# Expert 1's last twelve chunks, taken two by two over 768 tokens, with the first product by Strassen's algorithm

## The chip, the cores and the metric

The kernel runs on one core of one Trainium2 chip. The metric is the device time of one execution in microseconds (us); lower is better. Matrix products run on TensorE (PE in the profile), whose results land in eight PSUM banks of 128 x 512 floats. VectorE (DVE) and ScalarE (ACT) read and write the banks and SBUF. SyncE (SP) issues the transfers. On this kernel a change of less than 0.2% (1.2 us) can't be told from none.

## The reference

```python
x = attention(q, k, v)                 # 2 batches x 8 heads x 768 positions, head size 64
x = x.transpose(0, 2, 1, 3).reshape(1536, 512)
h = x @ w_in                           # expert 1: 512 -> 2048
x2 = (h * tanh(softplus(h))) @ w_out   # Mish, 2048 -> 512
a, b = x2 @ w_a, x2 @ w_b              # expert 2: 512 -> 1536, twice
return (a * b) @ w_out2                # 1536 -> 512
```

Each query attends to the keys less than 16 positions away and to 24 block summaries (maximum of the keys, mean of the values, over 32 positions). The weights come as 64-bit floats.

## The kernel before

Attention goes in 24 batches: six granules of 256 tokens by four pairs of heads. A granule of finished attention output is a piece of x. It is kept as two fp32r tiles, XH (rounded) and XL (what the rounding left), and so is every operand of the experts: a product w·x is three matmuls, wh·xh, wl·xh and wh·xl.

Expert 1 has 16 chunks of 128 hidden columns. A step (`step1`) takes one chunk for one block of tokens: 12 matmuls give h in one bank (L903), ACT makes Mish of it in SBUF (L932), a cast and a DVE subtraction (L388, L935) split the result, and 12 matmuls (L950) add to y, which stays in its four banks over all chunks of a visit. `visits1` gives the blocks of a visit and its chunks:

```python
visits1 = [((0,), 0, NG1), ((1,), 0, NG1), ((2,), 0, NG1),          # NG1 = 5
           ((3,), 0, NC1), ((2,), NG1, NC1), ((0, 1), NG1, NC1)]    # NC1 = 16
```

Blocks 0 and 1 have 256 tokens, blocks 2 and 3 have 512. So the chunks from 5 on come when much of attention is done, and each is used three times with 512 tokens. Converted weights stay in 26 slots of SBUF.

A weight tile (128 x 512) arrives as raw 64-bit halves. `convert` puts fp32 together from them: an ACT instruction (L685 or L688), DVE's shift L690, DVE's L693 and, where ACT's form is the unsigned one (L688), DVE's L697. `split` then needs an ACT cast (L388) and a DVE subtraction (L705).

Expert 2 already goes by Strassen's algorithm: for two 128-column products over half of the tokens (768, one batch), seven products of combined operands, six matmuls of 384 columns each (L1044), take the place of eight. Weight combinations come from DVE (L736), token combinations are made once per half (`combine_x`), and the seven results are put together by three ACT copies (L1052) and DVE operations on the banks (L1055). `expand` (L1105) is the last product, added up in SBUF by L1121.

No loop sets the order in which the engines work: all instructions are given to a planner (class `Plan`) with a key, the time at which each is due, and it writes out one order for each engine by keys, by readiness, by its own table of costs and by which banks are free. `pace` and the other constants are such keys. `tc.manual_schedule()` keeps that order.

Of the kernel before, what the change touches and what calls it, by code (L numbers as in the profile page):

```python
# [19 lines left out]
CELL = 32  # L20
# [212 lines left out]
def attention_mish_moe_bilinear_moe(  # L233
# [35 lines left out]
    n_blk = [GT, GT, 2 * GT, 2 * GT]  # L269
    t_blk = [0, GT, 2 * GT, 4 * GT]  # L270
    gran_blk = [(0, 0), (1, 0), (2, 0), (2, GT), (3, 0), (3, GT)]
# [5 lines left out]
    TOT, N_BASE, N_EXT = 53184, 16, 10  # L277
# [23 lines left out]
    NQ, NSA, NAT, NST, NT = 2, 4, 2, 3, 3  # L301
    XH = [take(KC * n) for n in n_blk]
    XL = [take(KC * n) for n in n_blk]
    G_HL = [take(1024) for _ in range(2)]
    base_slots = [take(1024) for _ in range(N_BASE)]
# [4 lines left out]
    kt_o = [take(SK) for _ in range(NP)]  # L310
    T_S = [take(512) for _ in range(NT)]
    T_L = [take(512) for _ in range(NT)]
    X2 = [Y0 + KC * GT * i for i in range(6)]
    assert Y1 == X2[1] and kt_o[0] == X2[2] and T_L[0] == T_S[0] + NT * 512
    TMP = X2[5] + KC * GT
    TN = 384
    tmp_o = [TMP + TN * i for i in range((T_L[-1] + 512 - TMP) // TN)]
# [15 lines left out]
    n_ext = max(top[0] - EXT, TOT - EXT, 1024 * N_EXT)  # L333
    assert EXT + n_ext <= TOT, EXT + n_ext
    ext_slots = [EXT + 1024 * i for i in range(N_EXT)]
# [3 lines left out]
    gran2 = {(0,): [0], (1,): [1], (2,): [2, 3], (3,): [4, 5], (0, 1): [0, 1]}  # L339
    XC = [{}, {}]  # L340
    XN = ("B11", "B21", "T2", "T1", "T3", "B22", "T4")

    def chunks(regions):
        out, rest = [], []
        for o, n in regions:
            while n >= 2 * TN:
                out.append((o, o + TN))
                o, n = o + 2 * TN, n - 2 * TN
            if n >= TN:
                rest.append(o)  # L350
        return out + list(zip(rest[0::2], rest[1::2]))

    SL = base_slots
    x_regions = [[(XH[0], 2048), (XL[0], 2048), (SL[3], 7 * 1024)], [(XH[2], 4096), (XL[2], 4096), (SL[0], 3 * 1024)]]
    assert XH[1] == XH[0] + 1024 and XL[1] == XL[0] + 1024 and XH[3] == XH[2] + 2048 and XL[3] == XL[2] + 2048
    for p_, rg in enumerate(x_regions):
        ch = chunks(rg)
        assert len(ch) >= 2 * len(XN), len(ch)
        for i_, nm in enumerate(XN):
            XC[p_][nm] = (ch[2 * i_], ch[2 * i_ + 1])  # L360

    b0, e0 = SL[10], EXT
    W2 = [b0, e0, e0 + 3584]
    O2 = [e0 + 7168 + 1024 * i for i in range(3)]
    PH = [G_HL[0], G_HL[0] + 768] + [b0 + 3584 + 768 * i for i in range(3)] + [e0 + 10240]
    assert b0 + 3584 + 3 * 768 <= SL[-1] + 1024 and n_ext >= 10240 + 768 and G_HL[1] == G_HL[0] + 1024

# [234 lines left out]
    def batch_o(key, g, ps):  # L602
# [60 lines left out]
        hk, lk = ([sb(X[blk] + p * n + t0, GT) for p in ps] for X in (XH, XL))  # L663
# [541 lines left out]
```

## Time and profile before

| | |
|---|---|
| median of 3 runs | 612.4 us (612.25 to 612.71) |
| profiled execution | 611.92 us, of which the span (first to last instruction) is 610.2 us |
| mean granted TensorE clock | 0.991 |
| PE busy | 597.1 us (98%) |
| PE weight loads busy | 525.4 us (86%) |
| DVE busy | 411.2 us (67%) |
| ACT busy | 295.9 us (48%) |

The busy shares are means over stages that differ: up to about 117 us attention and expert 1 are mixed, then come expert 1 alone (to 330 us) and expert 2. Busy time of neighbouring instructions overlaps, since one starts before the one ahead has finished; what an instruction costs its engine in a row is therefore the distance from its start to the next start. Lines are those of the kernel before; in the changed kernel the same code stands at other lines (L903 is L877 there, L950 is L923, L932 is L906, L935 is L909, L690, L693, L697 are L670, L673, L677, L705 is L685, L736 is L712, L634 is L615, L665 is L645, L1044 is L1052, L1105 is L1165).

### The profile page before, as it was taken

To read this page: it belongs to the slowest core of one execution; us is meant where nothing else is said; L and a number is where in the kernel's file an instruction comes from. 1 tells how busy PE (TensorE), PEld (TensorE's weight loads), DVE (VectorE), ACT (ScalarE), POOL (GpSimd) and SP (SyncE) were. 2 spreads that over 40 slices of the span, in tenths; PEclk is the share of its full clock that TensorE was granted. 3 is DMA by queue.
4 is the path that set the end of the run, shared out by engine and by line. 5 is a ranking of instruction groups with operands and counts; after the bars stand their busy time and mean duration, and the time that the engine had idled before them with its cause. 6 is when DMAs were issued, how large, how long until landed. Compare 5 with 4: busy or idle time off the path is not lost.

```text
span 610.2 us, 10411 instructions
## 1 busy us (share of the span) xinstructions
PE 597.1 (98%) x4119; PEld 525.4 (86%) x4119; DVE 411.2 (67%) x946; ACT 295.9 (48%) x648; POOL 6.8 (1%) x34
## 2 busy tenths in 40 slices
PE   7899999999999999999999999999999999999996
PEld 4688998888888888888888999999999999999995
DVE  5989999989831111148678865539879769656456
ACT  4889988766522322136356445345544524422210
POOL 3000000000000000000000000000000000000000
PEclk8979999999999999999999999999999999999999
DMA  8998432455500000001132012112342222000005
GB/s 301 337 317 271 143 102 71 144 196 172 180 1 0 1 0 1 1 1 40 64 119 89 1 35 70 36 69 70 105 137 70 69 70 71 0 35 1 0 1 207
DMA packets 20638, 54.87 MB, mean 90 GB/s; under 512 B 1805, under 2 KB 4877, under 8 KB 20589
## 3 DMA queue, kind: packets, MB, share of 16 engines
q1 hardware_dynamic: 20588, 54.21, 26.7%
q8 instruction: 32, 0.52, 0.4%
q14 instruction: 18, 0.14, 0.1%
HBM read 50.07 MB, written 3.15 MB: 87 GB/s over the span
## 4 chain that ended last, share of the span: by engine, by line
PE 90%; ACT 4%; DVE 2%; DMA 2%; issue 0%; SPq 0%; DVEq 0%; ACTq 0%
PE bank L1044 29%; PE bank L950 21%; PE bank L903 20%; PE bank L1105 16%; PE bank L634 2%; ACT attn L590 2%; PE bank L563 1%; PE bank L622 1%; DMA attn<-in_qT_dram 1%; ACT arena L688 1%; PE bank L567 1%; DMA out_dram<-arena 1%; ACT rounded L388 1%; DVE attn L584 0%; ACT L932 0%
## 5 line engine op out<-in xcount | busy, mean ns | idle before, releaser
L388 ACT CAST rounded<-arena 128x512 fp32r<-128x512 f32 (+3 forms) x139 | 82.4, 606 | 93.0 <-PE bank L950 40.3
L1044 PE MATMUL bank<-rounded,wext 128*128 128x384 f32 x672 | 120.4, 335 | 0.0
L1044 PEld LDWEIGHTS bank<-rounded,wext 128*128 128x128 f32 x672 | 117.1, 188 | 1.3 <-ACT arena L1052 0.5
L950 PE MATMUL bank<-rounded 128*128 128x512 f32 (+1 forms) x456 | 98.0, 364 | 0.0
L903 PE MATMUL bank<-rounded 128*128 128x512 f32 (+1 forms) x456 | 96.0, 363 | 0.5 <-ACT arena L932 0.5
L935 DVE TENSOR_TENSOR rounded<-arena,rounded 128x512 fp32r<-128x512 f32 (+1 forms) x53 | 33.8, 638 | 85.2 <-ACT rounded L388 85.0
L903 PEld LDWEIGHTS bank<-rounded 128*128 128x128 f32 x456 | 77.6, 189 | 14.4 <-ACT arena L932 0.7
L950 PEld LDWEIGHTS bank<-rounded 128*128 128x128 f32 x456 | 77.9, 189 | 13.7 <-issue 0.2
L1105 PE MATMUL bank<-wext,rounded 128*128 128x512 f32 x360 | 87.4, 390 | 0.0
L1055 DVE TENSOR_TENSOR arena<-arena,bank 128x384 f32<-128x384 f32 x96 | 52.6, 551 | 39.5 <-PE bank L1044 30.4
L1105 PEld LDWEIGHTS bank<-wext,rounded 128*128 128x128 f32 x360 | 67.4, 188 | 13.4
L705 DVE TENSOR_TENSOR rounded<-arena,rounded 128x512 fp32r<-128x512 f32 (+3 forms) x92 | 59.4, 658 | 5.7 <-ACT rounded L388 4.0
L1044 PE MATMUL bank<-rounded 128*128 128x384 f32 x336 | 61.1, 335 | 0.0
L1052 ACT COPY arena<-bank 128x384 f32<-128x384 f32 x72 | 34.3, 481 | 53.9 <-PE bank L1044 51.7
L1044 PEld LDWEIGHTS bank<-rounded 128*128 128x128 f32 x336 | 58.7, 188 | 0.6
L388 ACT CAST wext<-arena 128x512 fp32r<-128x512 f32 (+2 forms) x62 | 37.7, 615 | 43.3 <-DVE arena L1075 11.0
L932 ACT ACTIVATE arena<-bank 128x512 f32<-128x512 f32 (+1 forms) x53 | 29.4, 557 | 53.3 <-PE bank L903 53.2
L693 DVE SCALAR_TENSOR_TENSOR arena<-arena 128x512 uint32<-128x512 uint32 x68 | 47.0, 691 | 6.6 <-ACT arena L688 2.2
L1121 DVE TENSOR_TENSOR arena<-bank,arena 128x512 f32<-128x512 f32 x60 | 40.4, 687 | 14.1 <-PE bank L1105 13.5
L903 PE MATMUL bank<-rounded,wext 128*128 128x512 f32 x180 | 43.2, 389 | 0.0
L950 PE MATMUL bank<-rounded,wext 128*128 128x512 f32 x180 | 43.2, 389 | 0.0
L705 DVE TENSOR_TENSOR wext<-arena,wext 128x512 fp32r<-128x512 f32 (+2 forms) x62 | 38.7, 634 | 5.1 <-PE bank L950 2.5
(73 smaller groups left out, 566.9 us busy)
## 6 DMA issues: line engine op xcount, KB each, us to landing
arena<-in_w_out_dram SPq DMA_DIRECT2D x28, 512.0 KB, 3.3
arena<-in_w_in_dram SPq DMA_DIRECT2D x16, 512.0 KB, 4.2
arena<-in_w_a_dram SPq DMA_DIRECT2D x12, 512.0 KB, 3.2
arena<-in_w_b_dram SPq DMA_DIRECT2D x12, 512.0 KB, 3.7
arena<-in_kT_dram SPq DMA_DIRECT2D x8, 384.0 KB, 6.6
attn<-in_v_dram SPq DMA_DIRECT2D x4, 768.0 KB, 6.3
out_dram<-arena SPq DMA_DIRECT2D x12, 256.0 KB, 3.1
attn<-in_qT_dram SPq DMA_DIRECT2D x5, 512.0 KB, 6.1
```

What stands on the lines that cost most here:

```text
L388: alts = [("ACT", act_us(n), lambda env: nc.scalar.copy(out=dst(env), in_=src(env))), ("DVE", dve2_us(n) if fast else dve_us(n), lambda en ...
L693: dve(key, 512, lambda env: nc.vector.scalar_tensor_tensor(out=f.bitcast(U32), in0=hw.bitcast(U32), scalar=3, in1=f.bitcast(U32), op0=ALU. ...
L705: dve(key, n, lambda env: nc.vector.tensor_sub(out=r32(lo[0]()), in0=src, in1=hi[0]()), r=rd + hi[1], w=lo[1])
L903: nc.tensor.matmul(like(dst, b), lt, rt, start=(j == 0), stop=(j == 3 * KC - 1))
L932: act(ka, n, lambda env: nc.scalar.activation(out=g, in_=hp(env), func=AF.Mish), w=[hn, sb(lo, n)], free=[hn], table="mish")
L935: dve(ka, n, lambda env: nc.vector.tensor_sub(out=r32(gl), in0=g, in1=gh), r=[sb(lo, n), sb(ho, n)], w=[sb(go, n)])
L950: nc.tensor.matmul(yp, lt, r32(rt), start=(fst and j == 0), stop=(lst and j == 2))
L1044: nc.tensor.matmul(dst, lt, rt, start=(start and i == 0 and j == 0), stop=(last and i == 1 and j == 2), skip_group_check=True)
L1052: act(k, TN, lambda env: nc.scalar.copy(out=dst[0], in_=bank[env[nm[z]]][:, 0:TN]), w=[nm[z]] + dst[1])
L1055: dve(k, TN, lambda env: op(out=dst[0], in0=dst[0], in1=bank[env[nm[z]]][:, 0:TN]), w=dst[1] + [nm[z]], free=[nm[z]] if free else [])
L1105: nc.tensor.matmul(dst, lt, rt, start=(j == 0), stop=(j == n - 1))
L1121: dve(kf, 512, lambda env, acc=acc, ot=ot, on=on: nc.vector.tensor_add(ot, bank[env[on]], acc), r=ak, w=[on] + ok, free=[on])
```

## The change

Chunks 0 to 3 of expert 1 are still done block by block (`NG1 = 4`, four visits). Chunks 4 to 15 are done afterwards in pairs, for each pair first all 768 tokens of batch 0 (A), then all of batch 1 (B): twelve steps `step_l`. In each, h of both chunks comes from the routine for seven products that expert 2 uses (now `strassen`); four tiles of 128 x 384 go through Mish and are split; y comes in eight groups of six matmuls (both chunks, 384 tokens), and each group is added by DVE (L1128) to X2 in SBUF instead of waiting in a bank. The combinations of x that the seven products read are made by `combine_x1` (L974, L977) before the first step. Weights aren't kept: `prep_pair` prepares a pair of w_in chunks with Strassen's sums, double-buffered, and w_out goes through four slots. The choice between the two forms of `convert` goes by `SIGN`: the signed form early and late, the unsigned one (with the third DVE instruction) in between. Expert 2's order begins with half A instead of B.

```diff
-    NG1 = 5
-    visits1 = [((0,), 0, NG1), ((1,), 0, NG1), ((2,), 0, NG1), ((3,), 0, NC1), ((2,), NG1, NC1), ((0, 1), NG1, NC1)]
+    NG1 = 4
+    visits1 = [((0,), 0, NG1), ((1,), 0, NG1), ((2,), 0, NG1), ((3,), 0, NG1)]
-    pace = (6.2, 3.4, 5.2, 5.2, 5.2, 5.2)
+    pace = (6.2, 4.6, 6.0, 5.4)
+    D1 = 15.6
+    for cp in range(NG1, NC1, 2):
+        for p_ in (0, 1):
+            seqL.append((cp, p_, tl))
+            tl += D1
-        return w_first[c] > t + 20.0
+        return key < SIGN[0] or key > SIGN[1]
+    SIGN = (T0 + 20.0, tl + 20.0)
+    def step_l(cp, p_, ts):
+        e = IN[(cp - NG1) // 2 % 2]
...
+        def mish(nm, k, src, rd, o, free=()):
...
+            copy(k, TN, lambda env: r32(ar(o, TN)), lambda env: g, fast=True, r=gk, w=[sb(o, TN)])
+            dve(k, TN, lambda env: nc.vector.tensor_sub(out=r32(ar(o + TN, TN)), in0=g, in1=ar(o, TN)),
...
+        _, _, _, xn, _ = strassen(tag, p_, e, ts, d, out)
+        mish("21", ts + 7 * d, lambda env: bank[env[xn]][:, 0:TN], [xn], tmp(), free=[xn])
...
+        for j, (th, m) in enumerate((th, m) for th in (1, 0) for m in range(KC)):
...
+                for c, go, wa in pair:
...
+                    for lt, rt in ((wh, gh), (wl, gh), (wh, gl)):
+                        nc.tensor.matmul(bank[env[yn]][:, 0:TN], lt, rt, start=(q == 0), stop=(q == 5))
...
+            dve(k + 1.0, TN, lambda env, acc=acc, yn=yn: nc.vector.tensor_add(
+                acc, bank[env[yn]][:, 0:TN].rearrange("p (g n) -> p g n", g=3), acc), w=[yn] + ak, free=[yn])
+    combine_x1(A_, t - 16.0)
+    combine_x1(B_, t - 1.0)
+    for cp, p_, ts in seqL:
...
+            prep_pair(IN[i % 2], ts - (10.0 if i else 8.0), ("in", cp), ("in", cp + 1))
+            for c in (cp, cp + 1):
+                load_w(ts + 2.0 + 2.0 * (c - cp), "out", c, OUT[c % 4])
+        step_l(cp, p_, ts)
+    combine_x2(A_, tl - 10.0)
+    combine_x2(B_, tl + 12.0)
```

What this does to the orders is seen at three places. The first is TensorE around the last attention matmuls (the last AV product is the row on attn with 64x64). Before:

```order
L950 MATMUL bank_64<-rounded 128x512 x3
L950 MATMUL bank_67<-rounded 128x512 x3
L634 MATMUL bank_65<-attn 64x64 x16
L950 MATMUL bank_62<-rounded 128x512 x3
L950 MATMUL bank_63<-rounded 128x512 x3
L950 MATMUL bank_64<-rounded 128x512 x3
L903 MATMUL bank_68<-rounded 128x512 x12
```

In the changed kernel the same place reads:

```order
L615 MATMUL bank_65<-attn 64x64 x16
L923 MATMUL bank_66<-rounded 128x512 x3
L923 MATMUL bank_68<-rounded 128x512 x3
L923 MATMUL bank_61<-rounded 128x512 x3
L923 MATMUL bank_63<-rounded 128x512 x3
L877 MATMUL bank_67<-rounded 128x512 x12
```

and 120 matmuls of 512 columns after it, the first of the seven products begin:

```order
L923 MATMUL bank_68<-rounded 128x512 x3
L923 MATMUL bank_61<-rounded 128x512 x3
L1052 MATMUL bank_63<-rounded,wext 128x384 x6
L1052 MATMUL bank_62<-rounded,wext 128x384 x6
L1052 MATMUL bank_64<-rounded,wext 128x384 x6
L1052 MATMUL bank_65<-rounded,wext 128x384 x6
L1052 MATMUL bank_64<-rounded,wext 128x384 x6
```

Ahead of the last AV row stand 240 matmuls of 256 columns and 93 of 512 (L903, L950) before, 192 and 72 now. Behind it stand 939 of 512 and 1008 of 384 before, 120 and 2088 now, and 432 of L1105 (L1165) in both.

The second place is VectorE up to the subtraction that takes the last attention output from its bank (L665, now L645). Before, weight conversion stands there:

```order
L690 TENSOR_SCALAR arena<-arena 128x512
L693 SCALAR_TENSOR_TENSOR arena<-arena 128x512
L697 SCALAR_TENSOR_TENSOR arena<-arena 128x512
L705 TENSOR_TENSOR rounded<-arena,rounded 128x512
L665 TENSOR_TENSOR rounded<-bank_68,rounded 128x2x256
L705 TENSOR_TENSOR rounded<-arena,rounded 128x512
...
L665 TENSOR_TENSOR rounded<-bank_65,rounded 128x2x256
```

Now the combinations of x for half A stand there:

```order
L645 TENSOR_TENSOR rounded<-bank_62,rounded 128x512
L977 TENSOR_TENSOR arena<-rounded 128x384
L974 TENSOR_TENSOR rounded<-arena,rounded 128x384
L977 TENSOR_TENSOR arena<-arena 128x384 x2
L370 CAST rounded<-arena 128x512
L977 TENSOR_TENSOR arena<-arena 128x384
L909 TENSOR_TENSOR rounded<-arena,rounded 128x512
L974 TENSOR_TENSOR rounded<-arena,rounded 128x384
L974 TENSOR_TENSOR rounded<-arena,rounded 128x3x128
L645 TENSOR_TENSOR rounded<-bank_65,rounded 128x512
```

Counted over all rows from the start to this one, the changed VectorE has 7 fewer of L690, 9 fewer of L693, 17 fewer of L697 (none is left), 8 fewer of L705 and 2 fewer 256-column L935, and 23 more of 384 columns (L974, L977); it also has seven more casts and copies of 512 columns. ScalarE, counted up to its last cast of attention output, has four more table loads (15 for 11, and one at the start in both), 6 fewer weight conversions, 15 fewer casts and copies of 512 columns, 8 more casts of 384 and 3 fewer Mish.

The third place is TensorE in the steady part of the pairs, where a product and a y group alternate, each in a bank of its own:

```order
L1052 MATMUL bank_68<-rounded,wext 128x384 x6
L1121 MATMUL bank_65<-rounded,wext 128x384 x6
L1052 MATMUL bank_61<-rounded,wext 128x384 x6
L1121 MATMUL bank_63<-rounded,wext 128x384 x6
L1052 MATMUL bank_68<-rounded,wext 128x384 x6
L1121 MATMUL bank_62<-rounded,wext 128x384 x6
```

Before, twelve L903 and twelve L950 alternated here, and no bank was read between the steps but that of h.

## Rows read from the trace of the kernel before

**Rows 1.** The page: span, busy time of each engine, chain by engine.

```profile
span 610.2 us, 10411 instructions
PE 597.1 (98%) x4119; PEld 525.4 (86%) x4119; DVE 411.2 (67%) x946; ACT 295.9 (48%) x648; POOL 6.8 (1%) x34
PE 90%; ACT 4%; DVE 2%; DMA 2%; issue 0%; SPq 0%; DVEq 0%; ACTq 0%
```

**Rows 2.** The chain of waits, longest pieces: start us, us, what ran.

```profile
55.02 1.89 ACT attn L590 x10
58.64 1.28 ACT L932
60.38 1.70 PE bank L903 x12
62.08 1.44 PE bank L950 x12
...
116.12 1.08 PE bank L634 x32
117.20 2.27 PE bank L950 x9
119.46 2.72 PE bank L903 x12
...
308.50 5.44 PE bank L903 x24
...
330.26 28.16 PE bank L1044 x162
...
520.57 14.64 PE bank L1044 x84
...
601.75 3.23 DMA out_dram<-arena
```

**Rows 3.** Windows: stretch, its length, each engine's busy us (instructions), clock.

```profile
30.00:40.00 10.00, 8.09 (x148) 7.07 (x151) 9.19 (x21) 8.33 (x24) 0.00 (x0) 0.66 1.01 322
80.00:90.00 10.00, 10.00 (x131) 9.00 (x124) 10.00 (x50) 8.92 (x36) 0.52 (x1) 1.00 0.48 137
100.00:120.00 20.00, 20.00 (x167) 16.44 (x162) 19.04 (x54) 17.09 (x44) 0.00 (x0) 1.00 0.31 107
120.00:160.00 40.00, 40.00 (x178) 33.14 (x177) 36.03 (x65) 25.64 (x44) 0.00 (x0) 1.00 0.52 171
400.00:500.00 100.00, 100.00 (x523) 92.89 (x522) 80.99 (x161) 46.18 (x86) 0.00 (x0) 1.00 0.24 80
```

**Rows 4.** VectorE's timeline, three stretches: start us, busy us, instruction.

```profile
127.51 0.42 DVE L690 TENSOR_SCALAR arena<-arena 128x512 uint32<-128x512 uint32 x1
127.84 0.69 DVE L697 SCALAR_TENSOR_TENSOR arena<-arena 128x512 uint32<-128x512 uint32 x1
128.44 0.69 DVE L693 SCALAR_TENSOR_TENSOR arena<-arena 128x512 uint32<-128x512 uint32 x1
...
405.53 0.55 DVE L705 TENSOR_TENSOR rounded<-arena,rounded 128x384 fp32r<-128x384 f32 x1
405.99 0.55 DVE L1055 TENSOR_TENSOR arena<-arena,bank 128x384 f32<-128x384 f32 x1
406.46 1.29 DVE L705 TENSOR_TENSOR wext<-arena,wext 128x512 fp32r<-128x512 f32 x2
...
412.79 0.42 DVE L736 TENSOR_TENSOR arena<-arena 128x256 f32<-128x256 f32 x1
413.13 0.55 DVE L1075 TENSOR_TENSOR arena<-arena 128x384 f32<-128x384 f32 x1
```

**Rows 5.** ScalarE's timeline around a table load.

```profile
41.83 0.59 ACT L388 CAST rounded<-bank 128x512 fp32r<-128x512 f32 x1 [0.63 <-PE bank L634]
42.44 1.28 ACT L590 ACT_TABLE_LOAD   x1
43.73 0.40 ACT L590 ACTIVATE attn<-attn 128x120 f32<-128x120 f32 x1
```

More of the change, by code (lines that the diff above doesn't have):

```diff
@@ L299, in ar @@
         return a
[L301 to L305, printed above, removed]
+    NQ, NSA, NAT, NST, NT, SPARE = 2, 4, 2, 3, 3, 832
+    NG2 = S // GT * B
+    XH = [take(KC * GT) for _ in range(NG2)]
+    XL = [take(KC * GT) for _ in range(NG2)]
+    TE = [take(9 * 512) for _ in range(2)]
+    EW = [take(1024) for _ in range(8)]
+    G_HL = [TE[1], TE[1] + 1024]
     RND = top[0]
@@ L332, in attention_mish_moe_bilinear_moe @@
     st_o = [[take(GU) for _ in range(3)] for _ in range(NSA)]
-    n_ext = max(top[0] - EXT, TOT - EXT, 1024 * N_EXT)
+    n_ext = max(top[0] - EXT, N_EXT)
     assert EXT + n_ext <= TOT, EXT + n_ext
-    ext_slots = [EXT + 1024 * i for i in range(N_EXT)]
     PR = S
[L339 to L366, printed above, removed]
+    IN = [EXT, EXT + 3584]
+    OUT = [EXT + 7168 + 1024 * i for i in range(4)]
+    G1 = [EW[0] + 2 * TN * i for i in range(8)]
+    W2 = IN + [EW[0] + 6 * 2 * TN]
+    O2 = OUT[:3]
+    PH = [EW[0] + 2 * TN * i for i in range(6)]
+    assert W2[2] + 3584 <= EW[-1] + 1024
     rnd = sbuf.tile([P, RND], F32, name="rounded")
@@ L939, in step1 @@
         ky = ts + 2.2 * dt
-        first_of = lambda b: min(v[1] for v in visits1 if set(v[0]) & set(b))
         for m in range(KC):
@@ new lines, in packed, with operand @@
+    def packed(o, n=2):
+        a = ar(o, n * TN)
+        ap = bass.AP(a.tensor, a.offset, [a.ap[0]] + ([[TN, 2]] if n == 2 else []) + [[P, 3], [1, P]])
+        return ap, [sb(o, n * TN)]
+    X_IN = {"B11": (0, 0), "B21": (2, 0), "B22": (2, 1), "T3": (0, 1)}
+    X_EX = {"T1": 0, "T2": 1536, "T4": 3072}
+    def operand(p_, nm, i=None):
+        n, i = (2, 0) if i is None else (1, i)
+        if nm in X_IN:
+            kc, th = X_IN[nm]
+            return [tokens(X[3 * p_], kc + i, th, n) for X in (XH, XL)]
+        o = TE[p_] + X_EX[nm] + i * TN
+        return [packed(o, n), packed(o + 2 * TN, n)]
@@ new lines, in combine_x1, with whole @@
+    def combine_x1(p_, key):
+        add, sub = nc.vector.tensor_add, nc.vector.tensor_sub
+        for i in range(2):
+            def whole(k, nm):
+                o = nxt("early", early_o)[1]
+                out = packed(o, 1)
+                kc, th = X_IN[nm]
+                hi, lo = (tokens(X[3 * p_], kc + i, th, 1) for X in (XH, XL))
+                both(k, add, TN, out, hi, lo)
+                return out
+            k = key + 0.5 * i
+            b11, b12, b22 = (whole(k, nm) for nm in ("B11", "T3", "B22"))
+            t1 = packed(nxt("early", early_o)[1], 1)
+            both(k, sub, TN, t1, b12, b11)
+            keep_x(k, operand(p_, "T1", i), t1, TN)
+            both(k, sub, TN, b11, b22, t1)
+            keep_x(k, operand(p_, "T2", i), b11, TN)
+            both(k, sub, TN, b12, b22, b12)
+            keep_x(k, operand(p_, "T3", i), b12, TN)
+            b21 = whole(k, "B21")
+            both(k, sub, TN, b21, b21, b11)
+            keep_x(k, operand(p_, "T4", i), b21, TN)
```

216 lines of the change are left out of this document (116 added, 100 removed).

## The prediction

> **What bounds the kernel now.** I read the page first. PE is busy 98% of the span and holds 90% of the chain that ended last [rows 1], so the kernel is bound by TensorE unless a stage says otherwise. The chain in order of time says where: up to about 60 us its long pieces are ACT's and DVE's, from 60.38 us on only TensorE's, from the last attention matmuls (116.12 to 117.20) without a break to the last products, and then the final transfer [rows 2]. The windows say how the stages differ. Between 80 and 120 us DVE is busy 10.00 of 10 and 19.04 of 20 us, ACT 8.92 and 17.09, and PE all of it: three engines are nearly full, and PE is full partly because the planner fills its waits for attention with chunks of expert 1. In the early window 30 to 40 PE isn't full and its granted clock is 0.66, so part of it at 1.2 GHz, while DVE has 9.19 of 10. Behind attention DVE falls to 36.03 of 40, and in expert 2 it is at 80.99 of 100 [rows 3]. So I treat two parts by different rules: up to the end of attention the vector side sets the pace, behind it PE counts.
>
> **Behind the end of attention: matmuls counted.** The orders give 939 matmuls of 512 columns before against 120 now, and 1008 of 384 columns against 2088; the 432 of the last product stay. A 512-column one costs 2.72/12 = 0.2267 us, a 384-column one 28.16/162 = 0.1738 us [rows 2]. So 819 x 0.2267 = 185.7 us go and 1080 x 0.1738 = 187.7 us come: **+2.0 us**. This is not the whole count, since work that was ahead of the end of attention has moved behind it. For chunks 4 to 15 as a whole, 48 matmuls of 256 columns (1.44/12 = 0.120 us each [rows 2]) and 840 of 512 give way to the 1080: 5.8 + 190.4 - 187.7 = 8.5 us less on PE in all. What the change is worth therefore hangs on whether the first part gets shorter by the work that leaves it.
>
> **Ahead of the end of attention: three engines.** PE loses 48 matmuls of 256 columns and 21 of 512, 5.76 + 4.76 = 10.5 us. DVE: an instruction of 512 columns costs 128.44 - 127.84 = 0.60 us, the shift L690 127.84 - 127.51 = 0.33, one of 384 columns 405.99 - 405.53 = 0.46, one of 256 columns 413.13 - 412.79 = 0.34 [rows 4]. Gone are 7 x 0.33 + 9 x 0.60 + 17 x 0.60 + 8 x 0.60 + 2 x 0.34 = 23.4 us; added are 23 x 0.465 = 10.7 us for the combinations and 7 x 0.60 = 4.2 us for casts. Net **-8.5 us**. ACT loses 21 instructions of 512 columns at about 0.59 (12.4 us) and 3 Mish at about 0.4 (1.2), gains 8 casts of 384 columns (0.44 each, an estimate in proportion to the 0.59: 3.5) and four table loads, each 43.73 - 42.44 = 1.29 us from its start to the next start [rows 5], 5.2 in all: net -4.9 us. PE's saving alone isn't the answer, since PE waited for the others here; ACT's alone would hold if ACT were the fullest, which the windows 80 to 120 deny: DVE has the larger share in both. I take DVE's -8.5 and keep -4.9 and -10.5 as bounds. The end of attention would go from 117.2 to about 108.7 us.
>
> A rule speaks against this part. The Trainium skill (ScalarE: Activation LUTs, section What ACT_TABLE_LOAD costs) puts a change of tables at 2.66 us, about half of it a drain beyond the load of 1283 ns. The row agrees on the load (1.28) and doesn't show the drain behind it: the next activation starts 0.01 us after the load ends, and the instruction before ended 0.02 us ahead of it [rows 5]. By the page four more changes would cost 10.6 us instead of 5.2, and ACT's work ahead of the end of attention would grow by 0.5 us instead of falling.
>
> **The start of the pairs.** Behind the last attention matmuls PE has 120 matmuls of 512 columns, 27.2 us, before the first product. In that time DVE still makes the combinations of x for half B, the weights of the first pair and the splits of g. By the order these are about 27 us of DVE work at the rates above, so both arrive together. In the next 15 products (15.6 us of PE) DVE has about 17. Waits of one or two us can arise here; nothing if the planner's order happens to fit, up to 4 if the first product waits for the last split. I take 1.
>
> **Steady pairs.** A pair of chunks is 180 matmuls for both halves together, 31.3 us of PE. DVE has in it 30 instructions of 384 columns (six of the Strassen sums, eight splits of g, sixteen additions to X2): 30 x 0.465 = 14.0; and four weight tiles: 4 shifts (1.3), 13 of 512 columns (7.8), 5 of 256 (1.7). That is 24.8 us or 79%. ACT has less: 6 copies, 8 Mish and at most 8 casts at about 0.44, and four conversions with four and a half casts at 0.59, about 15. Expert 2 ran at 80.99 of 100 on DVE [rows 3] with 84 products in 14.64 us, 0.1743 each, against 0.1738 [rows 2]: the loss at this load was 0.3%. The y groups need a bank each, back after one DVE addition of 0.46 us, while PE needs 1.04 us for a group; with product and y alternating, DVE has about 2 us for each pair of them. I cost this stage at nothing beyond the count: the matmuls themselves cover the additions, and if the cover fails each step loses what DVE is late.
>
> **From the pairs to expert 2.** The token combinations of x2 for half A can only be made when its last y is added, and the first weights of expert 2 share the places of the last pair's. PE has half B's last y groups and products there, 14 groups or 14.6 us; DVE about 15. In the kernel before the same step (combinations of one half ahead, the other half's later) shows no break at 330.26 [rows 2], but there DVE had been nearly idle. Bounds 0 and 2; I take 1. Expert 2 behind it and the tail with its 3.23 us transfer stay [rows 2].
>
> **Sum.** Against the profiled 611.9 us (span 610.2 [rows 1], and 1.7 around it): -8.5 + 2.0 + 1 + 1 = -4.5, so 607.4. The median of the runs shown is 612.4, 0.5 above the profiled execution, so on it I forecast **607.9 us**. With DVE's term by its own uncertainty (-7 to -10) and the stalls from 0 to 4 the likeliest case spans 604.5 to 610.9.
>
> **The rivals.**
> *The pairs are bound by DVE (slower).* If a y addition or a split comes late once in each of the twelve steps and PE stands, say, 1 us each time (two additions of 0.46 with their handovers), the stage loses 12 us: 607.9 + 12 = 619.9. It outweighs the gain from 4.5/12 = 0.38 us a step on. For it: 79% load with more instructions in a chain (copy, addition, Mish, cast, split, y, addition) than expert 2 has, and banks that must return sixteen times a pair. Against it: the 0.3% loss above and DVE's 36.03 of 40 us at 120 to 160 with PE at 40.00 [rows 3]. Chance 0.18.
> *The end of attention is set by ACT (about the same).* Then it comes only 4.9 us earlier: 612.4 - 4.9 + 4 = 611.5. For it: the chain of 55 to 60 us runs through ACT, a table load among its pieces [rows 2]; four more loads come. Against: the windows behind. With a little less from the rest it is no change. Chance 0.17.
> *A table change costs as much again as its load (slower).* Then four more cost 4 x 1.29 more than I put down, ACT's part grows by 0.3 us instead of falling by 4.9, and if ACT also binds the time is 612.4 + 0.3 + 4 = 616.7. The row has no room for it. Chance 0.02. Much the same price is what the Trainium skill (ScalarE: Activation LUTs, What ACT_TABLE_LOAD costs) would give.
> *PE binds the first part and nothing waits later (more).* -10.5 + 2.0: 603.9. For it: PE is full from 80 to 120. Against: DVE is as full. Chance 0.11.
>
> **Chances and range.** The forecast case has 0.52. No change that can be told means within 0.2%, 611.2 to 613.6. Faster by more: 0.52 + 0.11 and a little of the ACT case, 0.64. Same: 0.15, most of the ACT case. Slower: 0.21, the DVE case, the table case and a rest. The range reaches down to the PE case, 603.5, and up over the ACT case and the mildest slower ones, to 613.
>
> **What would show it.** In the profile after: the last attention matmuls at 107 to 110 us (at 112 ACT was the bound, at 106 PE); no table load longer than 1.3 us to the next activation; 192 matmuls of 256 columns; the products and y groups at 0.174 to 0.176 us a matmul, with breaks of PE under 0.3 us a step; DVE at some 80% there; a break of about 1 us at the first product and one at the first product of expert 2. The prediction is wrong if PE's idle time in the pairs adds up to over 4 us, if attention ends later than 113 us, or if the 384-column matmuls of the pairs, whose moving operand now lies in three pieces of 128, take more than 0.178 us: 0.004 on 1080 of them is 4.3 us. No row of before has such an operand in the products; the nearest are the steps of the last visit, whose operand lies in two pieces of 256 in tiles apart: 5.44 us for 24, the same 0.2267 as all others [rows 2].

## The result, and the profile after

The changed kernel takes 605.57 us (median of 4 runs, 605.08 to 605.95) against 612.33 us for the kernel before on the same chip (612.19 to 612.71): ratio 0.9888, 95% interval 0.9871 to 0.9905. That is 6.8 us faster, where 4.5 were forecast; 605.57 lies in the range and within the span that the text gave to its likeliest case.

First the page of the changed kernel, the lines that answer to [rows 1].

```profile
span 603.7 us, 11060 instructions
PE 588.5 (97%) x4309; PEld 548.9 (91%) x4311; DVE 501.9 (83%) x1171; ACT 322.8 (53%) x721; POOL 6.7 (1%) x34
PE 75%; DVE 13%; ACT 5%; DMA 4%; issue 1%; SPq 0%; DVEq 0%; ACTq 0%
```

TensorE is busy 8.6 us less, near the 8.5 that the counted matmuls gave, and the span is 6.5 shorter: what TensorE stands idle has grown by 2, from 13.1 (610.2 - 597.1) to 15.2 us. VectorE has gone from 67% to 83%.

The chain of waits (start us, us, what ran) shows where the time was won; its rows answer to [rows 2].

```profile
46.62 7.09 DMA attn<-in_qT_dram
...
70.04 3.15 ACT attn L571 x16
77.37 1.08 PE bank L615 x32
...
107.09 1.08 PE bank L615 x32
108.17 2.95 PE bank L923 x12
111.12 2.72 PE bank L877 x12
...
124.72 10.88 PE bank L923 x48
135.60 7.31 PE bank L1052 x42
142.93 8.62 PE bank L1052 x48
151.55 9.36 PE bank L1121 x54
160.91 1.04 PE bank L1052 x6
161.95 1.04 PE bank L1121 x6
```

The last attention matmuls end at 108.17 instead of 117.20: 9.0 us. The first matmuls of 512 columns behind them cost a little more in both kernels (2.95 for twelve now, 2.27 for nine before [rows 2]), the next twelve take 2.72 in both, 48 take their 10.88, and the first seven products 7.31, so 0.1740 a matmul; in the steady pairs six take 1.04, 0.1733 each.

The rest of the account is read from TensorE's timelines. The kernel before, then the changed one, first matmuls behind the last attention ones and last of all:

```profile
117.13 1.66 PE L950 MATMUL bank<-rounded 128*128 128x512 f32 x6
602.41 2.20 PE L1105 MATMUL bank<-wext 128*128 128x512 f32 x9
```

```profile
107.02 1.15 PE L615 MATMUL bank<-attn 120*64 120x64 f32 x32
108.10 2.11 PE L923 MATMUL bank<-rounded 128*128 128x512 f32 x8
590.25 8.36 PE L1165 MATMUL bank<-wext,rounded 128*128 128x512 f32 x36
```

Behind attention TensorE works from 117.13 to 604.61 before, 487.5 us, and from 108.10 to 598.61 now, 490.5: 3.0 more, of which the count explains 2.0. Of the other 1.0 us, 0.4 is idle time of TensorE (it is busy 490.07 of the 490.51 us); the rest is no gap: TensorE is busy 2.6 us more where 2.0 were counted, so the 384-column matmuls cost 0.1743 us on the mean ((185.7 + 2.6) / 1080) instead of 0.1738. From the last matmul to the end of the span there were 5.6 us and are 5.1, 0.5 less. So -9.0 + 2.0 + 1.0 - 0.5 = -6.5, the difference of the spans.

Up to the end of attention, and behind it, TensorE's busy time reads as follows (a window each: its length, then busy us of PE, PEld, DVE, ACT and POOL; clock, DMA share, GB/s), first in the kernel before, then in the changed one:

```profile
0.00:117.13 117.13, 109.64 (x1741) 92.96 (x1741) 106.60 (x392) 96.85 (x294) 6.82 (x34) 0.96 0.66 214
```

```profile
0.00:108.10 108.10, 98.42 (x1669) 83.03 (x1671) 95.03 (x375) 90.80 (x280) 6.70 (x34) 0.97 0.61 198
108.10:598.61 490.51, 490.07 (x2644) 465.83 (x2640) 406.18 (x796) 232.03 (x441) 0.00 (x0) 1.00 0.19 66
```

So the 9.0 us are 11.2 us less of busy time on TensorE and 2.2 us more of idle time. The part can be divided further. The attention matmuls of the fourth of six granules end with the rows at 80.81 and 77.30, in the kernel before and in the changed one:

```profile
80.81 1.15 PE L634 MATMUL bank<-attn 120*64 120x64 f32 x32
116.05 1.15 PE L634 MATMUL bank<-attn 120*64 120x64 f32 x32
```

```profile
77.30 1.15 PE L615 MATMUL bank<-attn 120*64 120x64 f32 x32
```

The last granule ends at 116.05 and, in the row above, at 107.02. Between the two rows TensorE has no idle time in either kernel:

```profile
80.81:116.05 35.24, 35.24 (x412) 29.81 (x406) 34.52 (x122) 30.35 (x90) 0.52 (x1) 1.00 0.33 105
```

```profile
77.30:107.02 29.72, 29.72 (x383) 25.19 (x379) 28.95 (x117) 27.74 (x86) 0.52 (x1) 1.00 0.14 41
```

The stretch is 5.52 us shorter. In it stand 93 matmuls of 512 columns and 24 of 256 before, 72 and 18 now: 21 x 0.2267 + 6 x 0.120 = 5.48. So 5.5 of the 9.0 us are TensorE's own matmuls in the last two granules, and the other 3.5 arise before them.

The windows, answering to [rows 3] (stretch, its length, busy us of PE, PEld, DVE, ACT and POOL, then clock, DMA share, GB/s):

```profile
30.00:40.00 10.00, 6.88 (x187) 5.96 (x187) 9.64 (x28) 9.96 (x26) 0.00 (x0) 1.00 1.04 307
40.00:50.00 10.00, 10.00 (x96) 9.88 (x92) 8.24 (x43) 7.54 (x30) 0.51 (x1) 0.83 0.96 305
80.00:90.00 10.00, 10.00 (x140) 8.62 (x139) 9.59 (x33) 9.12 (x29) 0.00 (x0) 1.00 0.35 112
100.00:120.00 20.00, 20.00 (x146) 16.37 (x145) 19.65 (x44) 13.56 (x34) 0.00 (x0) 1.00 0.06 19
120.00:160.00 40.00, 39.97 (x209) 36.98 (x208) 39.69 (x82) 25.40 (x51) 0.00 (x0) 1.00 0.29 94
180.00:280.00 100.00, 100.00 (x578) 100.00 (x578) 86.51 (x177) 51.01 (x100) 0.00 (x0) 1.00 0.19 67
300.00:320.00 20.00, 20.00 (x117) 20.00 (x116) 18.75 (x31) 12.82 (x24) 0.00 (x0) 1.00 0.03 5
320.00:340.00 20.00, 20.00 (x118) 20.00 (x117) 19.44 (x36) 13.80 (x23) 0.00 (x0) 1.00 0.29 102
400.00:500.00 100.00, 99.79 (x529) 93.61 (x529) 82.96 (x166) 45.88 (x86) 0.00 (x0) 1.00 0.27 90
```

In the pairs (180 to 280) TensorE has no idle time, with VectorE at 86.5 of 100 us. At 120 to 160, where the pairs begin, VectorE has 39.69 of 40. From 80 to 90 us all three engines are over 90% busy, as TensorE and VectorE were before; from 30 to 40 us TensorE has only 6.88 of 10.

TensorE's granted clock has no large part in the 9 us: it was 0.66 from 30 to 40 us in the kernel before [rows 3] and 0.83 from 40 to 50 us in the changed one, so each ran a part of that at 1.2 GHz. The run l_dve3 below has the same work and order as the changed kernel up to the end of attention and ran all of it at 1.00; its last attention row starts 0.9 us earlier.

### The profile page after: what moved, and what is told of

It is laid out like the page before. It is cut to its first block, busy times and chain, and to the rows that moved or that the text cites. A ratio compares the mean times of both kernels' runs of the same rounds, so it can differ in the third digit from the quotient of the medians.

```text
span 603.7 us, 11060 instructions
## 1 busy us (share of the span) xinstructions
PE 588.5 (97%) x4309; PEld 548.9 (91%) x4311; DVE 501.9 (83%) x1171; ACT 322.8 (53%) x721; POOL 6.7 (1%) x34
## 4 chain that ended last, share of the span: by engine, by line
PE 75%; DVE 13%; ACT 5%; DMA 4%; issue 1%; SPq 0%; DVEq 0%; ACTq 0%
PE bank L1052 34%; PE bank L1165 15%; PE bank L1121 14%; PE bank L923 4%; PE bank L877 4%; DMA attn<-in_qT_dram 2%; DVE rounded L974 2%; ACT attn L571 2%; DVE arena L1065 2%; DMA arena<-in_w_out_dram 1%; PE bank L615 1%; DVE arena L673 1%; DVE rounded L685 1%; PE bank L603 1%; DVE wext L685 1%
## 5 line engine op out<-in xcount | busy, mean ns | idle before, releaser
L1052 PE MATMUL bank<-rounded,wext 128*128 128x384 f32 x1176 | 218.0, 335 | 0.1
L1052 PEld LDWEIGHTS bank<-rounded,wext 128*128 128x128 f32 x1176 | 205.5, 188 | 1.8 <-ACT arena L1061 0.5
L369 ACT CAST rounded<-arena 128x384 fp32r<-128x384 f32 (+3 forms) x153 | 83.6, 561 | 54.7 <-DVE arena L1135 24.2
L1121 PE MATMUL bank<-rounded,wext 128*128 128x384 f32 x576 | 110.1, 334 | 0.0
L1065 DVE TENSOR_TENSOR arena<-arena,bank 128x384 f32<-128x384 f32 x132 | 71.7, 549 | 38.5 <-PE bank L1052 31.2
L1165 PE MATMUL bank<-wext,rounded 128*128 128x512 f32 x432 | 100.9, 390 | 0.0
L1121 PEld LDWEIGHTS bank<-rounded,wext 128*128 128x128 f32 x576 | 100.8, 188 | 0.0
L1165 PEld LDWEIGHTS bank<-wext,rounded 128*128 128x128 f32 x432 | 80.9, 188 | 16.2
L369 ACT CAST wext<-arena 128x512 fp32r<-128x512 f32 (+1 forms) x80 | 49.0, 621 | 47.4 <-DVE arena L673 11.4
L1128 DVE TENSOR_TENSOR arena<-bank,arena 128x384 f32<-128x384 f32 x96 | 53.0, 552 | 9.3 <-PE bank L1121 8.9
L1052 PEld LDWEIGHTS bank<-rounded 128*128 128x128 f32 x336 | 58.5, 188 | 1.6 <-ACT arena L1061 0.8
L1181 DVE TENSOR_TENSOR arena<-bank,arena 128x512 f32<-128x512 f32 x60 | 40.3, 686 | 13.8 <-PE bank L1165 13.5
L685 DVE TENSOR_TENSOR wext<-arena,wext 128x512 fp32r<-128x512 f32 (+1 forms) x80 | 49.6, 637 | 0.6 <-ACT wext L369 0.3
L685 DVE TENSOR_TENSOR rounded<-arena,rounded 128x384 fp32r<-128x384 f32 (+2 forms) x72 | 40.8, 582 | 2.5 <-ACT rounded L369 1.9
L571 ACT ACTIVATE attn<-attn 128x120 f32<-128x120 f32 x96 | 36.7, 384 | 9.5 <-DVE attn L565 9.4
L923 PE MATMUL bank<-rounded 128*128 128x256 f32 (+1 forms) x192 | 38.9, 350 | 0.2 <-DVE rounded L685 0.2
L877 PE MATMUL bank<-rounded 128*128 128x256 f32 (+1 forms) x192 | 36.0, 340 | 0.2 <-DVE attn L574 0.2
L665 ACT ACTIVATE arena<-arena 128x512 f32<-128x512 f32 x38 | 25.8, 680 | 18.9 <-DMA arena<-in_w_a_dram 9.9
```

Of the source, the lines that this page charges most:

```text
L369: alts = [("ACT", act_us(n), lambda env: nc.scalar.copy(out=dst(env), in_=src(env))), ("DVE", dve2_us(n) if fast else dve_us(n), lambda en ...
L571: act(key, SW + 90, lambda env, x=x: nc.scalar.activation(out=s[:, x, :], in_=s[:, x, :], func=AF.Exp, scale=-1.0, bias=negm[:, x:x + 1], ...
L685: dve(key, n, lambda env: nc.vector.tensor_sub(out=r32(lo[0]()), in0=src, in1=hi[0]()), r=rd + hi[1], w=lo[1])
L877: nc.tensor.matmul(like(dst, b), lt, rt, start=(j == 0), stop=(j == 3 * KC - 1))
L923: nc.tensor.matmul(yp, lt, r32(rt), start=(fst and j == 0), stop=(lst and j == 2))
L1052: nc.tensor.matmul(dst, lt, r32(rt), start=(start and i == 0 and j == 0), stop=(last and i == 1 and j == 2), skip_group_check=True)
```

## The experiments

All runs are compared with the kernel before on their own chip. The chips of these runs spread more than the first one (the kernel before from 611.0 to 615.7), so differences below some 0.3% between two of them stay open; where a change sits is read from the profiles, one execution of each kernel. Up to the end of attention l_dve2 and l_dve3 do the same as the changed kernel, and their last rows start at 106.34 and 106.17, not 107.02: differences of "last AV" below 0.9 us can't be told from none. "Last AV" is the start of the last row of attention matmuls on TensorE's timeline, 116.05 in the kernel before and 107.02 in the changed one.

| run | median us | ratio to before (interval) | last AV, us | span, us |
|---|---|---|---|---|
| changed kernel | 605.57 | 0.9888 (0.9871 to 0.9905) | 107.02 | 603.7 |
| head_dve | 609.32 | 0.9938 (0.9913 to 0.9962) | 110.21 | 607.4 |
| head_act | 609.47 | 0.9945 (0.9926 to 0.9963) | 110.36 | 607.7 |
| head_pe | 607.66 | 0.9905 (0.9880 to 0.9929) | 110.05 | 606.7 |
| classic_h | 615.68 | 1.0045 (1.0027 to 1.0063) | 107.28 | 614.8 |
| no_wl | 604.55 | 0.9868 (0.9835 to 0.9901) | 105.74 | 602.5 |
| exp_g | 604.94 | 0.9876 (0.9832 to 0.9920) | 105.30 | 603.0 |
| light_dve | 604.34 | 0.9873 (0.9860 to 0.9887) | 106.47 | 603.0 |
| all_light | 596.86 | 0.9757 (0.9741 to 0.9773) | 98.19 | 595.0 |
| before_exp | 612.14 | 0.9999 (0.9982 to 1.0016) | 115.79 | 609.8 |
| l_dve2 | 623.29 | 1.0170 (1.0131 to 1.0210) | 106.34 | 621.4 |
| l_dve3 | 649.46 | 1.0597 (1.0563 to 1.0631) | 106.17 | 647.8 |
| keys_a | 604.63 | 0.9874 (0.9856 to 0.9892) | 103.88 | 600.4 |

Except for classic_h and keys_a these kernels keep every engine's order: an instruction is issued twice, left out or made cheaper where it stands, and the planner's costs aren't touched. Otherwise a new order would be measured along with the edit.

**Which engine ends attention: work added to one at a time.**

```diff
# head_dve: the subtraction of split, for the weights of chunks 0 to 3
-        dve(key, n, lambda env: nc.vector.tensor_sub(out=r32(lo[0]()), in0=src, in1=hi[0]()), r=rd + hi[1], w=lo[1])
+        dve(key, n, twice(lambda env: nc.vector.tensor_sub(out=r32(lo[0]()), in0=src, in1=hi[0]()), subs), ...
```

> The changed kernel with the order of all engines kept, and the subtraction that ends the preparation of each of the eight weight tiles of chunks 0 to 3 issued twice: 8 more instructions of 512 columns at 0.60 us, 4.8 us of VectorE work ahead of the end of attention, and nothing for the others. My theory (VectorE's work sets the end of attention there): the last attention matmul 4 to 5 us later and the time 605.6 + 4 to 5 = 609.6 to 610.6. Rival (TensorE or ScalarE sets it): 605.5 to 606.8.

```diff
# head_act: the cast of split, for the same weights
-        copy(key, n, lambda env: r32(hi[0]()), lambda env: src, only='ACT', r=rd, w=hi[1])
+        pl.add(key, [("ACT", act_us(n), twice(lambda env: nc.scalar.copy(out=r32(hi[0]()), in_=src), casts))], ...
```

> The changed kernel with the order of all engines kept, and the cast of each of the eight weight tiles of chunks 0 to 3 issued twice on ScalarE: 8 more casts of 512 columns at about 0.53 us, 4.2 us of ScalarE work ahead of the end of attention. My theory (VectorE sets the end): under 1.5 us more, 605.6 to 607. Rival (ScalarE sets it): 609.3 to 610.

```diff
# head_pe: x_product
+                if kk == 0 and b != (3,):
+                    for _ in range(3 if len(gran2[b]) == 1 else 2):
+                        nc.tensor.matmul(like(dst, b), wh, xh, start=True, stop=True)
```

> The changed kernel with the order of all engines kept, and the first matmul of h issued three more times in each step on 256 tokens and twice more in each step of chunks 0 to 3 on block 2: 24 more of 256 columns and 8 of 512, 24 x 0.12 + 8 x 0.227 = 4.7 us of TensorE work ahead of the end of attention. My theory (VectorE sets the end, TensorE has room by as much as it waits): 605.6 to 607.5. Rival (TensorE's count sets the whole time, since it is full from 80 us on): 609.8 to 610.5.

Attention ended later by 3.2 us for head_dve, by 3.3 for head_act and by 3.0 for head_pe. The first two added more than I had counted, since a repeat costs more than a row. VectorE's timeline of head_dve, then ScalarE's of head_act:

```profile
23.00 1.41 DVE L691 TENSOR_TENSOR rounded<-arena,rounded 128x512 fp32r<-128x512 f32 x2
24.32 0.42 DVE L645 TENSOR_TENSOR rounded<-bank,rounded 128x256 fp32r<-128x256 f32 x1
```

```profile
23.32 1.35 ACT L690 CAST rounded<-arena 128x512 fp32r<-128x512 f32 x2
24.57 0.37 ACT L369 CAST rounded<-bank 128x256 fp32r<-128x256 f32 x1
```

Two subtractions take 1.32 us, so the repeat 0.72 and eight of them 5.8 us instead of 4.8; two casts take 1.25, the repeat about 0.7 and eight of them about 5.5 instead of 4.2. Each engine passes on some 55 to 65% of what it is given, up to four fifths if l_dve2 and l_dve3 are taken as the start. The profiled execution of head_pe was the slowest of its four; by the medians it lost 1.5 us against the changed kernel (each compared with the kernel before on its own chip), where head_dve lost 3.2 and head_act 3.3. That contradicts the theory of the prediction, by which VectorE alone sets the end of attention.

Where the delay arises differs. All repeats of head_dve and head_act stand ahead of 65 us, and from the end of the fourth granule to the last row these two need 29.70 us, the changed kernel 29.72: the whole delay comes before. head_pe needs 31.51, 1.8 more, and its eight added matmuls of 512 columns count 8 x 0.227 = 1.8: in the last two granules TensorE passes on all of it. Of its 2.9 us ahead of them 1.2 come through.

**Work taken from one at a time.**

```diff
# no_wl: x_product (in y's product likewise)
-                for lt, rt in ((wh, xh), (wl, xh), (wh, xl)):
+                few = b != (3,)
+                for lt, rt in ((wh, xh), (wh, xl)) if few else ((wh, xh), (wl, xh), (wh, xl)):
```

> The changed kernel with all orders kept and the products wl·xh and wl·gh left out in the steps of chunks 0 to 3 on blocks 0, 1 and 2 (a third of their matmuls; the result lacks these terms): TensorE has 64 x 0.120 + 24 x 0.2267 = 13.1 us less ahead of the last attention matmul and 8 x 0.2267 = 1.8 less behind it. Theory after the first four runs (the three engines carry the part together, what is added to any goes through by two thirds, what is taken from one gains little, since the other two stay): attention ends 2 to 5 us earlier, time 599 to 602. Rival (TensorE's count alone): 13.1 + 1.8 less, 591.

```diff
# exp_g: step1
-        act(ka, n, lambda env: nc.scalar.activation(out=g, in_=hp(env), func=AF.Mish),
+        act(ka, n, lambda env: nc.scalar.activation(out=g, in_=hp(env), func=AF.Exp),
```

> The changed kernel with all orders kept and Exp in the place of Mish in the steps of chunks 0 to 3 (so another function is computed there): no change of tables is left in this part, 14 loads at 1.29 us, 18 us of ScalarE less. If ScalarE leads between 42 and 60 us, as the chain of before had it: attention ends 7 us earlier or more, time under 599. If the three engines are in balance: 2 to 5 us, 600.5 to 603.5. If VectorE or TensorE leads alone: 605 to 606.

```diff
# light_dve: attention's low part (g's and the weights' likewise)
-        dve(key, m, lambda env: nc.vector.tensor_sub(out=r32(x_of(XL)), in0=av(env), in1=x_of(XH)),
+        dve(key, m, lambda env: nc.vector.tensor_copy(r32(x_of(XL)), x_of(XH)),
```

> The changed kernel with all orders kept and the low parts of attention's output, of g and of the weights of chunks 0 to 3 made by a plain copy from SBUF instead of a subtraction (so they are not the remainders): VectorE has 8 x 0.27 + 10 x 0.27 + 4 x 0.14 for weights and attention and some 2.4 for g, about 7.5 us less ahead of the end of attention. If VectorE leads there: attention ends 4 to 7 us earlier, time 599 to 602. If no single engine does: 604 to 605.8.

Taking 13.1 us from TensorE brings the end of attention forward by 1.3 us, taking some 19 from ScalarE (15 loads at 1.29 stand ahead of the end of attention; I had counted 14) by 1.7, taking 7.5 from VectorE by 0.6, which can't be told from none. The last run was made because the first two left VectorE as the one leader; it isn't. I had expected 2 to 5 us of each of the first two; it is less.

In the last two granules exp_g needs 29.70 us and light_dve 29.72, so less work on ScalarE or VectorE changes nothing there, as where TensorE sets the pace. But no_wl needs 29.20, hardly less: once TensorE is lighter, the others hold it. Between 90 and 100 us of no_wl TensorE is busy 8.07 of 10, VectorE 10.00 and ScalarE 9.93:

```profile
90.00:100.00 10.00, 8.07 (x120) 6.27 (x119) 10.00 (x49) 9.93 (x35) 0.00 (x0) 0.91 0.01 2
```

The 1.8 us that no_wl saves behind the end of attention gain nothing either: from the last attention row to the end of the span it needs 496.8 us, the changed kernel 496.7.

**All three together.** The edits of the three runs above in one kernel.

> The three reductions together, orders kept: a third of the matmuls of chunks 0 to 3 on blocks 0 to 2 left out (13.1 us of TensorE ahead of the end of attention, 1.8 behind), Exp for Mish (18 us of ScalarE), low parts by copies (7.5 us of VectorE); the result is another one. If the three engines hold each other (each alone gave or should give next to nothing because the other two stay): attention ends at least 7 us earlier, at 101 or before, time under 598. If transfers or the fixed order itself set the pace: attention ends at 104 or later, time over 601.

Here the same rows read as follows, first the last attention matmuls on TensorE's timeline, then a window over 50 us:

```profile
98.19 1.15 PE L615 MATMUL bank<-attn 120*64 120x64 f32 x32
```

```profile
50.00:100.00 50.00, 47.63 (x876) 40.69 (x876) 48.85 (x203) 37.30 (x139) 0.52 (x1) 0.99 0.33 105
```

and the same window of the changed kernel:

```profile
50.00:100.00 50.00, 49.25 (x855) 43.67 (x854) 48.37 (x192) 48.62 (x142) 0.52 (x1) 1.00 0.36 117
```

Attention ends 8.8 us earlier, where the three alone sum to 3.6 (1.3 + 1.7 + 0.6), and the time is 8.7 us lower. In the changed kernel all three engines are between 48.4 and 49.3 of 50 us; that is why one alone gains so little. With less on all of them the part shrinks, though the order and the transfers are the same. 6.0 of the 8.8 us arise behind 58 us, where the third granule's first row stands in the changed kernel, so there neither transfers nor the order hold it; ahead of that, with the DMA share near 1 (1.04 from 30 to 40 us), transfers aren't ruled out. In the lighter kernel ScalarE has fallen to 37.30, and VectorE is the fullest. Whether two of the three reductions would have done wasn't tried.

**Was it ScalarE in the kernel before?** The changed kernel's lead is 0.8 us at the end of the second granule, 8.1 at the third's first row, 3.5 at the end of the fourth and 9.0 at the last. So the largest step lies between the second granule and the third, though more than half of it is given back, and there the chain of before runs through ScalarE from 42 to 60 us (55.02 and 58.64 in [rows 2]). That suggested a theory of its own: the change won there because ScalarE led there.

```diff
# the kernel before, step1: Mish -> Exp in all steps
-        act(ka, n, lambda env: nc.scalar.activation(out=g, in_=hp(env), func=AF.Mish),
+        act(ka, n, lambda env: nc.scalar.activation(out=g, in_=hp(env), func=AF.Exp),
```

> The kernel before with its orders kept and Exp in the place of Mish in all steps of expert 1 (another function): no change of tables is left in the part with attention, 11 loads of 1.29 us, four of them between 42 and 60 us, where the chain of before ran through ScalarE. Theory (the change won its time there, because ScalarE led there and had less to do): the attention output of the third granule (66.3 us in before) comes 4 to 5 us earlier, attention ends 3 to 6 earlier, time 606.5 to 609.5. Rival (no engine alone leads, as in the changed kernel, where the same edit gave 0.6): 611 to 612.5.

The last attention row starts at 115.79 instead of 116.05, and the time doesn't move. This theory falls too: 14 us of table loads less on ScalarE alone are worth 0.3 us, which can't be told from none; and the last two granules take 35.24 us as before. A chain through an engine says who came last, not what its work is worth. In the kernel before, ScalarE is the only engine whose work was lightened. There the chain runs on TensorE alone from 60.38 us on [rows 2], so that TensorE led there by itself is not ruled out.

**The part Strassen plays.** Pairs over 768 tokens and y in SBUF stay, but h comes from plain products.

```diff
# classic_h: step_l
-        _, _, _, xn, _ = strassen(tag, p_, e, ts, d, out)
-        mish("21", ts + 7 * d, lambda env: bank[env[xn]][:, 0:TN], [xn], tmp(), free=[xn])
+        for q, (th, c) in enumerate((th, c) for th in (1, 0) for c in (cp, cp + 1)):
...
+                for kk in range(KC):
+                    wh, wl = w_cols("in", c, kk)()
...
+                    for lt, rt in ((wh, xh), (wl, xh), (wh, xl)):
+                        nc.tensor.matmul(dst, lt, r32(rt), start=(j == 0), stop=(j == 11))
-    combine_x1(A_, t - 16.0)
-    combine_x1(B_, t - 1.0)
-    D1 = 15.6
+    D1 = 16.7
```

> The changed kernel with chunks 4 to 15 still in pairs over 768 tokens and y added up in SBUF, but h by plain products: 48 matmuls of 384 columns a step instead of 42, so 72 x 0.1738 = 12.5 us more on TensorE, and without the combinations of x (48 instructions of 384 columns on VectorE, 23 of them ahead of the end of attention, 10.7 us) and of the weights. My theory (VectorE sets the end of attention, these 23 count in it): 605.6 + 12.5 - 5 to 10.7 = 607.4 to 613. Rival (the combinations only fill VectorE's gaps, the products alone count): 617.5 to 618.5. Should the pairs have been held up by VectorE in the changed kernel, under 607.

The result lies between my theory and the rival. The span is 11.1 us longer, by the medians 9.5 to 10.1, of the 12.5 that the products count; what makes up the rest isn't shown. The last attention row stands at 107.28, 0.3 later, though 23 instructions of the combinations, 10.7 us by their distances, are gone from VectorE ahead of it. So they had cost nothing. Most of them stand in the last two granules, where TensorE has no idle time, and the others from 64 us on. Without Strassen the change is 0.45% slower than the kernel before; the new arrangement alone isn't worth anything.

**How much room VectorE has in the pairs.**

```diff
# l_dve2 (twice), l_dve3 (three times): step_l, mish
-            dve(k, TN, lambda env: nc.vector.tensor_sub(out=r32(ar(o + TN, TN)), in0=g, in1=ar(o, TN)),
-                r=gk + [sb(o, TN)], w=[sb(o + TN, TN)])
+            def low(env):
+                for _ in range(2):
+                    nc.vector.tensor_sub(out=r32(ar(o + TN, TN)), in0=g, in1=ar(o, TN))
+            dve(k, TN, low, r=gk + [sb(o, TN)], w=[sb(o + TN, TN)])
```

> The changed kernel with all orders kept and each subtraction that splits g in the pairs issued twice: 8 more instructions of 384 columns a pair, 48 in all, 3.7 us on VectorE for each 31.2 us of TensorE. My theory (in the steady pairs TensorE sets the pace, VectorE at 86% has room): 605.4 to 607. Rival (VectorE is the bound of the pairs or delays each step): 6 x 3.7 = 22 us more, 628.

> As the run before, three times each: 16 more a pair, 7.4 us. By the windows VectorE was busy 86.5 of 100 us, counting what lies beside its neighbour; by distances of starts some 25 of 31.2, so 32.6 now: over the edge by 1.4 us a pair, 6 x 1.4 = 8, and waits in the chain from h to y: 612 to 618. Rival as before: 650. If there is still room: under 607.

Both miss my expectation; 649.46 is close to the rival's 650, and 623.29 lies below its 628. But the rival was counted at 0.465 a repeat. The second issue costs more than its distance of 0.465, as VectorE's timeline of l_dve2 shows:

```profile
186.50 1.15 DVE L1102 TENSOR_TENSOR rounded<-arena,rounded 128x384 fp32r<-128x384 f32 x2
187.57 0.68 DVE L685 TENSOR_TENSOR wext<-arena,wext 128x512 fp32r<-128x512 f32 x1
```

The two take 1.07 us, so the repeat costs 0.60. 48 of them are 29 us, and the time grew by 17.7; 96 are 58 us, and it grew by 43.9. So 11 to 14 us were free over the six pairs, some 2 of 31.2 us a pair, 6 to 7%. The view of waits shows why VectorE's idle 13.5 us in 100 were not all free. In the changed kernel, 180 to 280 us (who waited for whom: us in total, times, longest):

```profile
DVE arena L1128 <- PE bank L1121: 7.0, 13, 1.3
DVE arena L1065 <- PE bank L1052: 3.0, 7, 0.6
DVE rounded L1100 <- ACT rounded L369: 2.3, 7, 0.7
```

and in l_dve2, where TensorE has to wait:

```profile
PEld bank L1124 <- DVE rounded L1102: 3.3, 4, 1.2
PE bank L1124 <- DVE rounded L1102: 3.0, 4, 0.9
```

VectorE in its fixed order waits for y's products and for casts in pieces of up to 1.3 us, which later work can't use up in full. So in the changed kernel VectorE doesn't bind the pairs, but the rival was only 2 us a pair away.

**Other due times.** Only the planner's numbers change:

```diff
# keys_a
-    TABLE, TABLE_PENALTY = 1.3, 14.0
+    TABLE, TABLE_PENALTY = 1.3, 7.51
-    T0 = 21.0
+    T0 = 19.78
-    pace = (6.2, 4.6, 6.0, 5.4)
+    pace = (6.57, 5.41, 5.07, 5.04)
-    SIGN = (T0 + 20.0, tl + 20.0)
+    SIGN = (T0 + 42.68, tl + 20.0)
-        out_t[g, p] = bt[g, p] + 8.0
+        out_t[g, p] = bt[g, p] + 7.81
-        kq, kw = ... (bt[g, 0] - 7.0, bt[g, 0] - 7.0)
+        kq, kw = ... (bt[g, 0] - 11.37, bt[g, 0] - 10.64)
-    combine_x1(A_, t - 16.0)
-    combine_x1(B_, t - 1.0)
+    combine_x1(A_, t - 18.0)
+    combine_x1(B_, t - -2.02)
```

> The changed kernel with other due times, found by trying numbers in the planner: T0 19.78, pace 6.57, 5.41, 5.07, 5.04, output of attention due 7.81 us after its start, q and the windows of v due 11.37 and 10.64 us ahead instead of 7, signed weights until T0 + 42.68, combinations due 18 us ahead and 2 us later, a lower penalty for a change of tables in the planner. The work is the same, but for the order. If the order of the first part leaves something: attention ends 1 to 2.5 us earlier, time 603 to 604.6. If not: 605 to 606.5.

In the profiled execution, the fastest of five, attention ends 3.1 us earlier and the span is 3.3 shorter; over the five runs (602.76 to 605.78) the median is 604.63, 0.9 below the changed kernel's, and the intervals of the two ratios overlap. The new order also has four table loads fewer (13 in all for 17). So a gain from the order is possible but not settled.

## Why the prediction was right, point by point

*Behind the end of attention, counted:* right. 0.1733 to 0.1740 us a matmul in the pairs, with moving operands in three pieces or not, and TensorE's busy time fell by 8.6 for 8.5. Over all of them the 384-column matmuls cost a little more than the row that was counted, 0.1743 for 0.1738, which makes 0.6 us.

*Ahead of the end of attention:* the size was right (-8.5 forecast, -9.0 measured), the reason wrong, so the hit is in part luck. The step that failed is "I take DVE's -8.5": VectorE alone doesn't set that part. What the runs show in its place: in the last two granules TensorE sets the pace in both kernels, and its count there, 5.48, is the 5.52 us that were won; less work on ScalarE or VectorE changes nothing in that stretch (exp_g, light_dve, before_exp), and work added to TensorE comes through in full (head_pe). The other 3.5 us arise in the first four granules, where TensorE's idle time grew by 2.2 us and where work added to any of the engines delays the end. The combinations, put down at +10.7 us, cost nothing (classic_h). In the changed kernel a reduction on one engine alone is worth little, since the other two are close behind, and on all three it is worth 8.8 us (all_light). That the change gained because it took work from all three, 10.5 us from TensorE, some 5 from ScalarE and more from VectorE, fits this but was not shown on the kernel before, where only ScalarE was lightened by itself. The bounds from the three engines held the value: -9.0 lies between VectorE's -8.5 and TensorE's -10.5.

*The start of the pairs,* put at 1: next to nothing. The first product starts at 135.60, 0.2 us after 108.17 + 27.2, and the first twelve matmuls behind attention, with 2.95 for 2.72, account for that. *The step to expert 2,* put at 1: no gap, TensorE is busy 20.00 of 20 us from 300 to 320 and from 320 to 340. Both terms were mis-sized. All idle time behind attention is 0.44 us, most of it two waits in expert 2:

```profile
PE bank L1052 <- ACT arena L1061: 0.2, 1, 0.2
PE bank L1052 <- DVE arena L1065: 0.2, 1, 0.2
```

VectorE, at 39.69 of 40 us where the pairs begin, did arrive together with TensorE, as the orders had it: in no_wl, with 1.8 us less on TensorE there, TensorE stands idle for 1.6.

*Steady pairs at nothing:* right in time, TensorE 100.00 of 100. The room was mis-sized: 79% for VectorE was forecast, leaving 21%, and 6 to 7% could be used. The sum of distances left out the waits of a fixed order.

*The tail,* taken as unchanged, gave 0.5 us.

*The sum:* the likeliest case was said to span 604.5 to 610.9; its terms (-7 to -10 for VectorE, 0 to 4 for the stalls) give 604.4 to 611.4 on 612.4. The measured 605.57 lies in both.

*The rivals:* pairs bound by VectorE didn't come about, by about 2 us a pair. ScalarE setting the end of attention was wrong in both kernels (exp_g, before_exp). TensorE setting it alone was wrong for the changed kernel as a whole (no_wl), though it sets the last two granules; for the kernel before it wasn't tried. Its forecast of 603.9 was missed by 1.7 us, the likeliest case's 607.9 by 2.3. That a table change costs more than its row: four more of them stood in a part that got 9.0 us shorter, and taking all 15 out gave 1.7, all 11 in the kernel before 0.3. By the Trainium skill (ScalarE: Activation LUTs, What ACT_TABLE_LOAD costs) the 15 would be 40 us of ScalarE, an estimate from its 2.66 us a change. The row shows 1.29, so 19 us [rows 5], and not even the 19 were on the path by themselves.

## What to carry to other kernels

Where several engines are each 95% full, ask what a change takes from all of them: taking 13 us from one gave 1.3, taking from three at once 8.8, and adding to any one passed on more than half. Divide such a part further before naming what sets it: where one engine has no gap over a stretch, count its instructions there, and see whether the stretch moves when another engine gets less. Issuing an instruction twice with the order kept is a cheap probe for that, and for the room that a stage has left; a busy share is no measure of room when the engine's order is fixed. Helper work that a scheduler can place beside the engine that sets the pace, here the combinations of x beside TensorE's matmuls, may cost nothing even on an engine that looks full. And what a repeat costs is read from the repeat itself: here it cost a fifth to a third more than the row it was counted from.

## What was not expected of the hardware

A VectorE subtraction of 384 columns issued twice in a row to the same output took 1.07 us for both, against 0.465 from start to start for instructions on different data in the kernel before [rows 4]: the repeat cost 0.60 us, a little more than the busy time of one, 0.55. At 512 columns (head_dve) the repeat cost 0.72, against 0.60 from start to start and 0.69 busy.
